# A long-convolution kernel: spectrum rows with real and imaginary part side by side, one transfer per chunk's multiplier, and taps stored in partition order

## The chip, the cores and the metric

The kernel runs on one core of a Trainium2 chip. The metric is device time in microseconds (us) of one execution; lower is better. A core has five engines that run side by side, each with its own instruction queue that is worked through in order: TensorE (PE, matrix products; PEld is its weight load), VectorE (DVE), ScalarE (ACT), GpSimd (POOL) and SyncE (SP). SP computes nothing here: it issues almost every transfer between the chip's DRAM and the on-chip memory, which has 128 partitions. The transfers themselves are carried out by 16 DMA engines; the profile's "DMA share" is the mean busy share of these 16.

## The reference

`x` has 2048 positions and 512 channels. Four layers are applied in turn, A, B, A, B, with the same weights for both A layers and both B layers, each added to `x`.

```python
def _A_ref(q, k, v, shift_k, ssm_k, ssm_D):      # q = layernorm(x)
    kv = shift_conv(k, shift_k) * v              # 4 taps per channel
    y = irfft(rfft(kv, 4096) * rfft(ssm_k, 4096))[:2048]
    return q * (y + kv * ssm_D)

def _B_ref(u, ...):                              # u = layernorm(x)
    K = 2 * real(sum_n C[d, n] * exp(A[d, n] * dt[d] * l))   # 512 channels x 2048 taps
    y = irfft(rfft(u, 4096) * rfft(K, 4096))[:2048]
    return y + u * D_skip

x = x + _A_ref(layernorm(x), ...); x = x + _B_ref(layernorm(x), ...)
x = x + _A_ref(layernorm(x), ...); x = x + _B_ref(layernorm(x), ...)
```

So there are long convolutions with two sets of filters, done as a product of spectra. The convolution in A does not depend on `x` (only its gate does), so it is computed once and used in both A layers. The convolution in B runs twice.

## The kernel before

**Tiling.** The 512 channels are handled in 4 quarters `q` of 128, each quarter in 4 groups `g` of 32. A 4096-point transform is done as two steps of small matrix products on TensorE. Step one (`pf`, line 177) is followed by a 32x32 block transpose on DVE; step two (`pu`, line 206, in `f2_pair`) gives the spectrum in 8 chunks `c` per quarter. A chunk is a block of 128 partitions by 4 residues by 128 channels. Of the 128 partitions one half belongs to a residue of one kind and the other half to the other kind; within a half, 32 rows hold real parts and the next 32 rows hold imaginary parts. The table `w2` sets this order. The way back is `i1_pair` (`pi`, line 221, with the table `mm`), a copy on ACT (line 341), a transpose on DVE (`w`, line 355) and a last product (`po`, line 361).

**The filters' spectra.** `spectrum_quarter` transforms the filter taps in the same way and stores the result chunk by chunk in DRAM (`spec`, line 290). For A (`which == 0`) the taps are an input. For B (`which == 1`) `taps()` computes them, group by group, with ACT, DVE, POOL and PE; `contract` scales them into a tile `ks` (lines 578 and 579), stores them to `kdram` (line 581), and `spectrum_quarter` loads them back into the tile `kk` (line 265). This last load goes through `by_half` (line 227): the positions in DRAM are in the order (a, b, n) and the tile wants (b, a, n), so it is done as two transfers of 64 partitions, and the DRAM side of each is a pattern of 2 blocks by 32 rows. `by_half` also loads the other inputs (`kk` for A, `kvt`, `xt`, `xr`) and stores the result (`out`, line 921).

**The convolution.** `convolution` runs through 32 chunks (4 quarters by 8). For each chunk, `load` (line 299) brings the filter's spectrum into a tile `kab` with two halves: `kab[:, 0]` are the rows as stored, `kab[:, 1]` the same rows with real and imaginary parts exchanged. The first takes one transfer of 256 KB (line 305), the second four of 64 KB (line 309). Then DVE forms `vv = pu * kab[:, 0]` (line 329), ACT copies `pu` (line 327) and POOL multiplies the copy by `kab[:, 1]` (line 328, `sw`). The matrix `mm` puts the four products of real and imaginary parts together with the right signs while it does the first inverse step. The inverse of a chunk pair runs `lag` chunks later, and the last inverse step another 8 chunks later; at its end `finish_b` (line 908) adds the result to `x` and, in the last layer, stores it.

**What sets the order.** The tile framework lets a program write tiles; it places the waits and, by its own simulation of the engines, orders the instructions of each queue. A tile name has a fixed number of buffers, and a new tile waits until the oldest is free: `kab` has 4 buffers in B (`NKB`) and is loaded 3 chunks ahead (`AHB`), 3 buffers and 2 chunks ahead in A; `yo`, the output tile in the last layer, has 3. Completion of a transfer issued on SP is counted on one of 8 counters in turn, and a transfer that gets a counter waits on SP until the one that had it before is done.

**Stages.** Up to about 466 us: inputs for A are loaded, A's filters are transformed, `kv` is formed, and the taps of B begin. From about 530 to 860 us: A's convolution, with B's taps running beside it; the taps end at about 917 us. From 942 us: B for the first time ("the first B round"). From about 1050 us: the second A layer, which is only its gate. From 1098 us: B for the second time ("the second B round").

## Time and profile before

| | |
|---|---|
| median of 3 runs | 1252.41 us (1247.11 to 1254.38) |
| the profiled execution, its own time | 1260.55 us |
| its span in the trace | 1258.7 us |
| busy: PE, PEld, DVE, ACT, POOL | 693.5, 453.6, 582.5, 412.8, 389.0 us |
| mean granted TensorE clock | 0.718 |
| moved by DMA | 147.49 MB in 93626 packets |
| issues of `kab <- spec` on SP | 94 of 256 KB and 376 of 64 KB |
| issues of `kk <- kdram` on SP | 32 of 128 KB |

No engine is busy for more than 55% of the span, so the time is not read from these shares but stage by stage. The views used below: "windows" give the busy time of each engine in a stretch, with instruction counts, the granted clock, the DMA share and the bytes moved; "timeline" lists the instructions of one engine in order (start, duration, what; in brackets the idle time before and what ended it); "waits" sum the idle time of an engine by what it waited for; "the chain of waits" follows the work that ended last back from its end. An issue on SP is shown as SPq with the time that the issuing took. The profiled execution lasted 8.1 us longer than the median.

### The profile page before, as it was taken

The numbers are of one execution on the slowest core, as the hardware profiler recorded it, in microseconds if no ns is written. First come the engines' busy times: TensorE is split into PE (matmuls) and PEld (weight loads), VectorE is DVE, ScalarE is ACT, GpSimd is POOL, SyncE is SP. The second block draws the span as 40 slices with busy tenths as digits, with TensorE's granted clock in tenths as the row PEclk, the third lists the DMA queues.
The fourth block names the chain that finished last, engine by engine and source line by source line (L and its number), as shares of the span: only waits on it lengthen the run. The fifth ranks groups of instructions, "written<-read, shape, count | busy, mean of one in ns | idle before, by whom it ended". The sixth has DMA issues, their size and how long they took to land. (4 is left out here: it accounts for less than half of the span.)

```text
span 1258.7 us, 21783 instructions
## 1 busy us (share of the span) xinstructions
PE 693.5 (55%) x8648; PEld 453.6 (36%) x8648; DVE 582.5 (46%) x995; ACT 412.8 (33%) x755; POOL 389.0 (31%) x371
## 2 busy tenths in 40 slices
PE   1220334143445455882455989987648884786651
PEld 0120213022323233551232757654435552354430
DVE  3320132445534323551215648786615668964330
ACT  2100131031213121571234454657325334752210
POOL 2331233443323211451113335432324341242220
PEclk9555566556656556796676979896768897897885
DMA  4112331222222233362335556446236763063431
GB/s 131 73 65 99 125 119 59 90 69 78 88 95 74 71 111 113 107 179 72 98 106 167 180 162 197 123 154 178 68 124 185 212 201 106 14 203 116 133 93 48
DMA packets 93626, 147.49 MB, mean 117 GB/s; under 512 B 12492, under 2 KB 41684, under 8 KB 90964
## 3 DMA queue, kind: packets, MB, share of 16 engines
q1 hardware_dynamic: 92532, 143.68, 35.7%
q0 software_dynamic: 992, 2.43, 0.6%
q8 instruction: 68, 1.11, 0.4%
q14 instruction: 34, 0.28, 0.1%
HBM read 102.01 MB, written 44.04 MB: 116 GB/s over the span
## 5 line engine op out<-in xcount | busy, mean ns | idle before, releaser
L328 POOL TENSOR_TENSOR sw<-sw,kab 128x512 f32<-128x512 f32 x96 | 121.9, 1276 | 293.9 <-DMA kab<-spec 155.4
L177 PE MATMUL pf<-kk,wz 128*128 128x256 f32 x256 | 106.2, 568 | 185.4 <-DMA kk<-ssmk_in 60.8
L206 PE MATMUL pu<-zk,w 64*64 64x128 f32 x1024 | 74.3, 349 | 137.6 <-ACT pc L289 95.2
L177 PEld LDWEIGHTS pf<-kk,wz 128*128 128x128 f32 x256 | 66.6, 281 | 213.7 <-issue 106.2
L329 DVE TENSOR_TENSOR vv<-pu,kab 128x512 f32<-128x512 f32 x96 | 64.1, 683 | 143.8 <-ACT sw L327 89.3
L289 ACT COPY pc<-pu 128x512 f32<-128x512 f32 x64 | 36.5, 587 | 284.1 <-DMA spec<-pc 174.2
L221 PE MATMUL pi<-vv,mm 64*64 64x128 f32 x1536 | 113.5, 289 | 6.7 <-DVE vv L329 4.2
L554 POOL TENSOR_TENSOR xy<-tt,m 128x512 f32<-128x512 f32 x64 | 86.8, 1356 | 91.7 <-issue 53.2
L206 PEld LDWEIGHTS pu<-zk,w 64*64 64x64 f32 x1024 | 58.0, 174 | 156.8 <-ACT pc L289 99.3
L221 PE MATMUL pi<-sw,mm 64*64 64x128 f32 x1536 | 109.7, 283 | 1.8 <-issue 1.6
L206 PE MATMUL pu<-zu,w 64*64 64x128 f32 x1536 | 90.0, 313 | 32.3 <-DVE yo L919 15.1
L206 PEld LDWEIGHTS pu<-zu,w 64*64 64x64 f32 x1536 | 72.0, 155 | 62.1 <-DVE vv L329 17.9
L660 DVE TENSOR_TENSOR u<-kvt 128x512 f32<-128x512 f32 x15 | 10.4, 693 | 175.7 <-DMA kvt<-kv_in 147.7
L221 PEld LDWEIGHTS pi<-vv,mm 64*64 64x64 f32 x1536 | 77.0, 141 | 36.9 <-issue 12.0
L327 ACT COPY sw<-pu 128x512 f32<-128x512 f32 x96 | 53.6, 590 | 97.9 <-PE pu L206 97.6
L541 ACT ACTIVATE tt<-pa 128x512 f32<-128x512 f32 x64 | 38.3, 601 | 139.6 <-PE pa L533 130.4
L661 POOL TENSOR_TENSOR tb<-kvt 128x512 f32<-128x512 f32 x16 | 27.6, 1728 | 177.3 <-DMA kvt<-kv_in 177.3
L221 PEld LDWEIGHTS pi<-sw,mm 64*64 64x64 f32 x1536 | 79.7, 141 | 4.3 <-issue 3.7
L197 DVE STREAM_TRANSPOSE zk<-pf 128x512 f32<-128x512 f32 x64 | 44.3, 703 | 67.3 <-PE pf L177 67.3
L361 PE MATMUL po<-w,w 128*64 128x512 f32 x192 | 59.0, 705 | 25.9 <-DVE vv L329 19.1
L569 PE MATMUL pk<-xy,tt 128*32 128x64 f32 x2048 | 58.5, 258 | 24.3 <-POOL tb L661 13.2
L518 ACT ACTIVATE m<-pm 128x512 f32<-128x512 f32 x96 | 54.2, 598 | 51.5 <-PE pm L516 50.2
(144 smaller groups left out, 1289.8 us busy)
## 6 DMA issues: line engine op xcount, KB each, us to landing
kab<-spec SPq DMA_DIRECT2D x94, 256.0 KB
kab<-spec SPq DMA_DIRECT2D x376, 64.0 KB
spec<-pc SPq DMA_DIRECT2D x64, 256.0 KB
kvt<-kv_in SPq DMA_DIRECT2D x32, 312.0 KB
kk<-ssmk_in SPq DMA_DIRECT2D x32, 128.0 KB
xr<-x_in SPq DMA_DIRECT2D x8, 512.0 KB
kv_d<-u SPq DMA_DIRECT2D x16, 256.0 KB
kdram<-ks SPq DMA_DIRECT2D x64, 64.0 KB
```

Source lines behind the costliest of these rows:

```text
L177: yield T.matmul(o, w, rhs, start=True, stop=True)
L197: V.transpose(zr, both)
L206: ins = T.matmul(pus[odd][64 * o:64 * o + 64, i, :], w2[64 * h:64 * h + 64, k, :], z[64 * h:64 * h + 64, :, k, :], start=True, stop=True, ...
L221: ins = T.matmul(pis[odd][64 * o:64 * o + 64, i, :], mm[64 * h:64 * h + 64, k + i, 64 * part:64 * part + 64], w[part][64 * h:64 * h + 64, ...
L327: swapped[0] = S.copy(wb, pu)
L328: G.tensor_mul(wb, wb, kabs[s][:, 1])
L329: V.tensor_mul(wa, pu, kabs[s][:, 0])
L361: ins = T.matmul(po[64 * a:64 * a + 64], w4, ws[g][:, :, 16 * a:16 * a + 16, :].rearrange("p x t r -> p t x r"), start=True, stop=True, ti ...
L518: i = S.activation(m, pm, AF.Exp)
L541: S.activation(co, rv, AF.Abs)
L554: G.tensor_mul(xy[:, :, :, 32:64], tt[:, :, :, 1:33], m1[:, :, 32:64][:, None].to_broadcast([128, 2, 8, 32]))
L569: T.matmul(pk[32 * i4:32 * i4 + 32, 2 * k + i, :], e2[:, r, 4 * i + i4, :], xy[:, r, 4 * i + i4, :], start=r == 0, stop=r == 1, tile_posit ...
```

## The change

Three things are changed together.

1. **Order of rows in the spectra.** In `w2` (and in `mm`, which takes the products apart again) the index of real or imaginary part is now innermost: rows 2f and 2f+1 are the real and the imaginary part of one frequency f. This order holds for the signal's spectrum (`pu`) and for the filter's (`spec`).
2. **One transfer per chunk's multiplier.** `kab[:, 0]` is now the filter's real part in both rows of a frequency, `kab[:, 1]` its imaginary part in both rows. So `vv = pu * Kre` and `sw = pu * Kim`, and `mm` has other signs and positions. In DRAM the two rows of a frequency lie one behind the other, 4096 bytes in all, and both rows of the tile get these same 4096 bytes. One transfer does it, with a source pattern of 64 by 2 (step 0) by 1024 elements; it moves 512 KB, as the five did.
3. **Taps in partition order.** `contract` writes `ks` so that the taps arrive in `kdram` in the order (b, a, n) of the partitions. The two multiplications keep their 256 elements per partition, with one more dimension in the pattern. `kk` is then loaded for B by one transfer of 128 partitions.

```diff
--- before.py
+++ after.py
@@ -35,8 +35,8 @@
     pos = (2 * n1[None, :] + a[:, None]).reshape(64)
     w1 = np.zeros((64, 2, 2, 32))
     w4 = np.zeros((2, 2, 32, 64))
-    w2 = np.zeros((2, 2, 32, 32, 2, 32))
-    mm = np.zeros((2, 2, 32, 32, 2, 2, 32))
+    w2 = np.zeros((2, 2, 32, 32, 32, 2))
+    mm = np.zeros((2, 32, 2, 32, 2, 2, 32))
     for k in range(32):
         for s in range(2):
             if k == 0 and s == 0:
@@ -46,13 +46,13 @@
                 for i in range(32):
                     r = i // 16
                     th = 2 * np.pi * ((128 * i if r == 0 else 64 + 128 * (i - 16)) * j % NFFT) / NFFT
-                    w2[0, r, :, 0, 0, i] = np.cos(th)
-                    w2[0, r, :, 0, 1, i] = -np.sin(th) if i else (-1.0) ** j
+                    w2[0, r, :, 0, i, 0] = np.cos(th)
+                    w2[0, r, :, 0, i, 1] = -np.sin(th) if i else (-1.0) ** j
                     if i == 0:
-                        mm[0, 0, 0, 0, 0, 0], mm[0, 1, 0, 0, 0, 0] = 1, (-1.0) ** j
+                        mm[0, 0, 0, 0, 0, 0], mm[0, 0, 1, 0, 1, 0] = 1, (-1.0) ** j
                     else:
-                        mm[0, 0, i, 0, 0, r], mm[0, 1, i, 0, 0, r] = 2 * np.cos(th), -2 * np.cos(th)
-                        mm[0, :, i, 0, 1, r] = -2 * np.sin(th)
+                        mm[0, i, 0, 0, 0, r], mm[0, i, 1, 0, 0, r] = 2 * np.cos(th), -2 * np.sin(th)
+                        mm[0, i, 0, 0, 1, r], mm[0, i, 1, 0, 1, r] = -2 * np.sin(th), -2 * np.cos(th)
                 continue
             f = k + 64 * s if k else 32
             ang = 2 * np.pi * (f * pos % 128) / 128
@@ -60,11 +60,13 @@
             w4[s, 0, k], w4[s, 1, k] = 2 * np.cos(ang) / NFFT, -2 * np.sin(ang) / NFFT
             th = 2 * np.pi * ((f + 128 * q)[None, :] * j[:, None] % NFFT) / NFFT
             co, si = np.cos(th), np.sin(th)
-            w2[s, 0, :, k, 0], w2[s, 0, :, k, 1] = co, -si
-            w2[s, 1, :, k, 0], w2[s, 1, :, k, 1] = si, co
-            mm[s, 0, :, k, 0, 0], mm[s, 0, :, k, 0, 1] = co.T, si.T
-            mm[s, 1, :, k, 0, 0], mm[s, 1, :, k, 0, 1] = -co.T, -si.T
-            mm[s, :, :, k, 1, 0], mm[s, :, :, k, 1, 1] = -si.T, co.T
+            w2[s, 0, :, k, :, 0], w2[s, 0, :, k, :, 1] = co, -si
+            w2[s, 1, :, k, :, 0], w2[s, 1, :, k, :, 1] = si, co
+            co, si = co.T, si.T
+            mm[s, :, 0, k, 0, 0], mm[s, :, 0, k, 0, 1] = co, si
+            mm[s, :, 1, k, 0, 0], mm[s, :, 1, k, 0, 1] = -si, co
+            mm[s, :, 0, k, 1, 0], mm[s, :, 0, k, 1, 1] = -si, co
+            mm[s, :, 1, k, 1, 0], mm[s, :, 1, k, 1, 1] = -co, -si
     for c in range(1, NCH, 2):
         odd = slice(CK * c, CK * c + CK)
         mm[:, :, :, odd] = mm[::-1, :, :, odd].copy()
@@ -262,7 +264,10 @@
         nc.sync.dma_start(dr, (ssmd_in, dsk_in)[which][:, 128 * q:128 * q + 128])
         for g in range(4):
             kk = pool.tile([128, 512], F32, name="kk", tag="kk", bufs=(NKK, 2)[which])
-            by_half(kk, src[4 * q + g])
+            if which == 0:
+                by_half(kk, src[4 * q + g])
+            else:
+                nc.sync.dma_start(kk, src[4 * q + g])
             d = dr[:, 32 * g:32 * g + 32]
             if which == 0:
                 kv = kk.rearrange("p (t c) -> p t c", c=32)
@@ -301,12 +306,8 @@
             pool = pools["conv"]
             kab = pool.tile([128, 2, CK, 128], F32, name="kab", tag="kab", bufs=nk)
             eng = G if first_b and s < GL else nc.sync
-            rows = spec[which][q][c]
-            eng.dma_start(kab[:, 0].rearrange("p k c -> p (k c)"), rows)
-            for r in range(2):
-                for h in range(2):
-                    o = 64 * h + 32 * r
-                    eng.dma_start(kab[o:o + 32, 1].rearrange("p k c -> p (k c)"), rows[64 * h + 32 - 32 * r:64 * h + 64 - 32 * r])
+            rows = spec[which][q][c].rearrange("(f v) x -> f (v x)", v=2)
+            eng.dma_start(kab.rearrange("p v k c -> p (v k c)"), rows[:, None, :].to_broadcast([64, 2, 2 * CK * 128]))
             kabs[s] = kab
 
         for s in range(-2 * NCH, NS + lag + NCH + 1):
@@ -573,10 +574,11 @@
             return
         q, g = divmod(gi, 4)
         ks = wk.tile([128, 64, 8], F32, name="ks", tag="ks", bufs=2)
-        d2 = dt2[:, q, 8 * g:8 * g + 8][:, :, None].to_broadcast([128, 8, 32])
-        kv_ = ks.rearrange("p n c -> p c n")
-        V.tensor_mul(kv_[:, :, 32:64], pk[:, :, 0:32], d2)
-        V.tensor_mul(kv_[:, :, 31::-1], pk[:, :, 32:64], d2)
+        d2 = dt2[:, q, 8 * g:8 * g + 8][:, :, None, None].to_broadcast([128, 8, 2, 16])
+        kv_ = ks.rearrange("p (b a t) c -> p a c b t", b=2, a=2)
+        halves = lambda m0: pk[:, :, m0:m0 + 32].rearrange("p c (b t) -> p c b t", b=2)
+        V.tensor_mul(kv_[:, 1], halves(0), d2)
+        V.tensor_mul(kv_[:, 0, :, ::-1, ::-1], halves(32), d2)
         for i4 in range(4):
             nc.sync.dma_start(
                 kdram[gi].rearrange("(s n) (i x) -> i n s x", n=32, i=4)[i4],
```

What is issued on the queues changes with it. The number of transfers of `kab <- spec` falls from 480 (470 on SP, 10 on POOL) to 96 (94 and 2), that of `kk <- kdram` from 32 to 16. Line numbers move by one to five. The order on SP at three places follows; a row is a line of the program, the operation, the tiles (left the destination) and the shape of the destination, and x2 stands for two in a row.

**SP, before the last loads of `xt`.** `xt` are the rows of `x` from which the first layernorm's sums are taken, and the stage up to 466 us ends with them. Before:

```order
L231 DMA xt<-x_in 64x1x512 x2
L290 DMA spec_3_60<-pc 128x512
L231 DMA xt<-x_in 64x1x512
L670 DMA kv_d_97<-u 128x512
L290 DMA spec_3_60<-pc 128x512
L231 DMA xt<-x_in 64x1x512 x5
L309 DMA kab<-spec_0_57 32x512
L305 DMA kab<-spec_0_57 128x512
```
Now:

```order
L233 DMA xt<-x_in 64x1x512 x2
L672 DMA kv_d_97<-u 128x512
L233 DMA xt<-x_in 64x1x512 x2
L295 DMA spec_3_60<-pc 128x512
L270 DMA kk<-kdram_67 128x512
L295 DMA spec_3_60<-pc 128x512
L233 DMA xt<-x_in 64x1x512 x2
L295 DMA spec_3_60<-pc 128x512
L233 DMA xt<-x_in 64x1x512 x2
L270 DMA kk<-kdram_68 128x512
L295 DMA spec_3_60<-pc 128x512
L233 DMA xt<-x_in 64x1x512
```
Two loads of `kk` from `kdram` (the groups 67 and 68) that came after the last `xt` now stand among the last ones; each is one row of 128 partitions.

**SP, end of the taps.** `kdram_80` is the last group of taps; its spectrum (`spec_3`) is stored, and then the first B round's loads begin. Before:

```order
L581 DMA kdram_79<-ks 32x4x128 x4
L231 DMA kk<-kdram_79 64x1x512 x2
L581 DMA kdram_80<-ks 32x4x128 x4
L231 DMA kk<-kdram_80 64x1x512 x2
L290 DMA spec_3_64<-pc 128x512 x8
L305 DMA kab<-spec_0_61 128x512
L309 DMA kab<-spec_0_61 32x512 x4
```
Now:

```order
L583 DMA kdram_79<-ks 32x4x128 x4
L270 DMA kk<-kdram_79 128x512
L583 DMA kdram_80<-ks 32x4x128 x4
L270 DMA kk<-kdram_80 128x512
L295 DMA spec_3_64<-pc 128x512 x8
L310 DMA kab<-spec_0_61 128x1x1024 x6
```
The order of the steps is the same; each load of `kk` is one issue, and the loads of `kab` that follow are one issue each.

**SP, the second B round, around the first stores of the result.** Before:

```order
L305 DMA kab<-spec_2_63 128x512
L309 DMA kab<-spec_2_63 32x512 x4
L305 DMA kab<-spec_2_63 128x512
L309 DMA kab<-spec_2_63 32x512 x4
L231 DMA out_dram<-yo 2x32x512 x2
L305 DMA kab<-spec_2_63 128x512
L309 DMA kab<-spec_2_63 32x512 x4
L305 DMA kab<-spec_2_63 128x512
L309 DMA kab<-spec_2_63 32x512
L231 DMA out_dram<-yo 2x32x512 x2
L309 DMA kab<-spec_2_63 32x512 x3
L231 DMA out_dram<-yo 2x32x512 x2
```
Now:

```order
L310 DMA kab<-spec_0_61 128x1x1024 x4
L310 DMA kab<-spec_1_62 128x1x1024 x8
L310 DMA kab<-spec_2_63 128x1x1024 x2
L233 DMA out_dram<-yo 2x32x512 x2
L310 DMA kab<-spec_2_63 128x1x1024 x2
L233 DMA out_dram<-yo 2x32x512 x4
L310 DMA kab<-spec_2_63 128x1x1024 x2
L233 DMA out_dram<-yo 2x32x512 x2
```
The stores keep their two issues per group (by halves). Ahead of the first store stood ten issues for two chunks, now two.

## The prediction

> **What bounds the kernel now.** I read the windows by stage first: time, the five engines' busy time, granted clock, DMA share, GB/s.
>
> ```profile
> 0.00:466.00 466.00, 159.48 (x1237) 101.48 (x1238) 165.40 (x216) 84.64 (x142) 148.46 (x143) 0.59 0.25 90
> ...
> 680.00:860.00 180.00, 158.81 (x2149) 106.44 (x2149) 132.24 (x247) 96.78 (x171) 72.16 (x69) 0.89 0.49 158
> 860.00:942.00 82.00, 49.99 (x563) 36.13 (x564) 35.09 (x65) 35.40 (x70) 23.59 (x29) 0.68 0.40 117
> 942.00:1036.00 94.00, 77.46 (x1390) 51.98 (x1388) 58.27 (x106) 41.58 (x87) 37.01 (x30) 0.89 0.66 202
> ...
> 1098.00:1259.00 161.00, 92.62 (x1580) 60.94 (x1578) 62.02 (x84) 40.70 (x80) 42.18 (x34) 0.80 0.39 119
> ```
>
> Only from 680 to 860 us is an engine near full: PE, 159 of 180 us. Up to 466 us no engine passes 36%. The two B rounds do nearly the same work (1390 and 1580 products), yet one takes 94 us for its chunks and the other 161 us to the end. So three stages wait for something that is no engine. What it is, narrow windows and issues show:
>
> ```profile
> 303.00:313.00 10.00, 10.00 (x83) 5.29 (x82) 5.56 (x9) 4.31 (x8) 2.35 (x2) 0.70 0.14 54
> 1242.00:1258.00 16.00, 0.00 (x0) 0.00 (x0) 0.69 (x1) 0.00 (x0) 0.00 (x0) 0.50 0.12 48
> 274.98 6.03 SPq L231 DMA_DIRECT2D kk<-kdram  x2
> 456.11 10.23 SPq L231 DMA_DIRECT2D xt<-x_in  x5
> kvt<-kv_in SPq DMA_DIRECT2D x32, 312.0 KB
> kk<-ssmk_in SPq DMA_DIRECT2D x32, 128.0 KB
> xt<-x_in SPq DMA_DIRECT2D x32, 128.0 KB
> ```
>
> Where transfers by halves (`by_half`) run alone, loads at 303 us or the last stores from 1242 us, the DMA share stays at 0.12 to 0.14: 0.125 is two engines of sixteen, and they move 48 to 54 GB/s. A pair of halves, 256 KB, thus holds two engines for 4.9 to 5.5 us. The three loads by halves before 466 us (32 x 312 KB and 64 x 128 KB, 18.6 MB) need 345 to 390 us at that rate, and an issue on SP takes microseconds there since SP waits for earlier transfers. **The early stage is bound by two DMA engines.** The first B round shows another picture in the chain of waits (start, duration, what):
>
> ```profile
> 963.85 0.36 SPq L305
> 964.25 0.43 SPq L309
> 964.72 0.42 SPq L309
> 965.18 0.42 SPq L309
> 965.65 0.42 SPq L309
> 966.18 0.36 SPq L305
> POOL sw L328 <- DMA kab<-spec: 58.2, 23, 15.9
> DVE vv L329 <- DMA kab<-spec: 18.3, 9, 5.2
> ```
>
> One chunk's five issues take 2.33 us (963.85 to 966.18), with stalls 94/32 = 2.94 us, and the chain runs through them issue after issue; POOL and DVE wait for `kab` (the last two rows, the waits from 930 to 1060 us: in total, times, longest). **The first B round is bound by SP's issuing.** The second round has both: the same issues, and the stores by halves among them.
>
> ```profile
> 1126.78 0.65 DVE L919 TENSOR_TENSOR yo<-x,po 128x512 f32<-128x512 f32 x1
> 1135.98 1.15 SPq L231 DMA_DIRECT2D out_dram<-yo  x2
> 1145.38 0.69 DVE L919 TENSOR_TENSOR yo<-x,po 128x512 f32<-128x512 f32 x1 [7.77 <-DMA out_dram<-yo]
> DVE yo L919 <- DMA out_dram<-yo: 33.6, 5, 8.2
> SPq L309 <- DMA out_dram<-yo: 12.8, 8, 3.8
> ```
>
> The first `yo` is done at 1127.4, but its store is issued at 1136.0, behind ten issues of `kab`; the fourth `yo` wants its buffer and DVE stands 7.8 us, with PE behind it. Loads wait for stores in turn, since there are 8 counters.
>
> **The change, part by part.** All sums are against the profiled execution (1260.55 us, of which 1258.7 us span); it lies 8.1 us above the median, and I carry the difference over to the median unchanged.
>
> *Products and rows.* `vv` and `sw` keep their shapes, `w2` and `mm` theirs: 0. The two scalings of the taps get a pattern with one more dimension:
>
> ```profile
> L578 DVE TENSOR_TENSOR ks<-pk,dt x16: 580/613/654, 268.7 to 916.8; 128x256 f32<-128x256 f32 x16
> L579 DVE TENSOR_TENSOR ks<-pk,dt x16: 623/640/681, 269.1 to 917.2; 128x256 f32<-128x256 f32 x16
> ```
>
> The second is already the odder pattern (it writes backwards) and costs 27 ns more. I take 0; if every one of the 32 grew by half its time it would be 10 us of DVE, of which only the last group's 0.6 us lies on the chain.
>
> *One load of `kk` for two halves (16 pairs).* The last groups stand on the chain, with nothing beside them:
>
> ```profile
> 899.58 7.00 DMA kk<-kdram
> 921.61 7.54 DMA kk<-kdram
> POOL kk L275 <- DMA kk<-kdram: 60.8, 12, 11.1
> PE pf L177 <- DMA kk<-kdram: 30.9, 6, 12.6
> 907.20 3.75 PE L177 MATMUL pf<-kk,wz 128*128 128x256 f32 x8 [5.09 <-DMA kk<-kdram]
> SPq L581 <- DVE ks L579: 46.5, 7, 17.7
> kab<-spec POOLq DMA_DIRECT2D x2, 256.0 KB, 3.2
> kab<-spec POOLq DMA_DIRECT2D x8, 64.0 KB, 2.6
> ```
>
> A 256 KB transfer over 128 partitions landed in 3.2 us when POOL issued it; SP's own have no landing time, so I take 3.2. That gives 3.8 + 4.3 = **8 us** at the end of the taps (bounds 4, if the load at 899 is covered by the taps' ACT work, and 9). Before 466 us two pairs go off the two engines: 2 x (4.9 - 0.6, the same bytes over sixteen) = 8.6; but SP also stands for the taps themselves (46.5 us at line 581), when the two engines can run dry, so **7 us** (0 to 9); the two loads that now stand ahead of the last `xt` cost 0.6 us each. Of the ten pairs between, PE waited 30.9 - 12.6 - 5.1 = 13 us; half of that goes: **6 us** (0 to 13). What is late next there is `xr` and PE itself, which stays full from 680 to 860 us.
>
> *One load of `kab` for five.* SP's 2.33 us per chunk become one issue. Nearest rows: 0.36 us for 128 rows, and 1.30 us for the only load with a repeated dimension, made among others at the start:
>
> ```profile
> L467 SPq DMA_DIRECT2D dt<-ldtb_in x1: 1302/1302/1302, 4.4 to 4.4; - x1
> ```
>
> I take 0.4, by the row of nearer shape; even 1.3 is under PE's share of a chunk. So SP leaves the chain of the first B round, and the next bound is PE, at full clock:
>
> ```profile
> 1116.93 0.88 PE pu L206 x32
> 1117.81 1.06 PE pf L177 x4
> 1118.87 1.92 PE pi L221 x64
> 1041.38 1.08 PE po L361 x4
> ```
>
> 16 pairs x 3.86 + 16 groups x 1.08 = 79 us against 94. The transfers need 32 x 512 KB / 202 GB/s = 83 us at today's share of 0.66, so some 55 us when full. PE will not run without gaps (the clock in this stage was 0.89): **10 us** (0 to 17, the latter PE's busy 77.5 of 94). POOL's eight issues less at 927 us lie beside the last taps' load: 0. `vv` now waits for 512 KB, no longer for the first 256; with loads 3 chunks (8 us) ahead this is covered, and without that cover it costs 0.8 us per chunk (2.6 and 3.2 us for 64 and 256 KB give 4.0 for 512).
>
> A rule speaks against this term. The Trainium skill, "DMA: Bandwidth & Descriptors", section "Issuing engines are not separate DMA queues", says that the time a sequencer needs to start a DMA is usually small beside the DMA itself. By it the SP terms of both B rounds would be nothing and the sum 21 instead of 44. Here the rows above have 2.33 us of issue beside 2.6 us of data per chunk (512 KB at 202 GB/s), so I go by the rows.
>
> *Second B round.* Stores remain by halves. The first `yo` comes at about 1125 (1126.8 less a stall of `vv`), is stored at once, and from there the two engines carry 16 x 5.5 = 88 us of stores and some 16 chunks x 32 KB at 24 GB/s each = 22 us of loads: 1125 + 110 + 2 = 1237 if they never idle. Before, 1136 + 88 + 14 x 1.37 = 1243 stands against 1258.7, 16 us of idling. I keep half of that idling: 1246, **13 us** (0 to 23). What is late next are the two engines.
>
> *A's convolution* (560 to 860 us): its loads of `kab` shrink too, but PE or `xr` is the bound there: 0 (-8 to 8, since the order on all queues shifts).
>
> Sum: 8 + 7 + 6 + 10 + 13 = 44 us: 1260.6 - 44 = 1216.6 profiled, and 1252.4 - 44 = **1208** for the median.
>
> **Rivals.**
>
> *Only the bare waits* (chance 0.20): the two engines set the early stage and the second B round whatever SP does, and gaps elsewhere close up. Left are 8 at the taps' end and 10 in the first round: 1234 us. For it: the stores keep their halves. Against it: the 8.6 us by which the first store came late.
>
> *All bounds met* (0.13): 9 + 9 + 13 + 17 + 23 + 5 (A) = 76, 1176 us. For it: PE's idle time behind SP is plain in both rounds. Against: it needs PE without gaps.
>
> *Both products wait for one landing* (0.06): place `vv` and `sw` in all 96 chunks, price 0.8 us each, 77 us; less the 44 it is +33, 1285 us. It decides from the point at which a load is issued less than 4 us before its chunk's `pu` is copied. For it: `vv` waits for `kab` today (9 times in the first round). Against: those waits come from SP's issuing.
>
> *The load does not spread* (0.03): like the halves, the new source has a dimension of 2, and if it ran on two engines a chunk would take 512 KB / 54 GB/s = 9.7 us instead of 2.9, some 650 us more over three rounds, 1900 us. Against: in the halves the 2 is outermost, here 64 is. The Trainium skill, the same page, section "Why a DMA increments its semaphore by 16 and not by 1", says that the number of engines is the largest up to 16 that divides the slowest dimension of both sides; by it the halves get 2 and this load 16. For the halves the trace agrees (0.12 to 0.14); for a load of this shape no run here shows it yet.
>
> **How the numbers follow.** The forecast has 0.58; its own range from the bounds is 1186 to 1228. 8 in 10 need the first rival and most of the second: 1176 to 1242. A measurement of this kernel tells about 0.5% (6 us) from no change. Faster: all of the forecast but 0.02, 0.17 of the first rival, the second: 0.86. Same: 0.05. Slower: the two last rivals: 0.09.
>
> **What would show it.** Right: issues of `kab` of about 0.4 us and gaps between them on SP from 942 us; POOL's and DVE's waits for `kab` in the first round (58 and 18 us) mostly gone, PE without idle time; `kk` landing in 3 to 4 us on the chain; the first store within 2 us of its `yo`; the window after the last `yo` still at 0.12. Wrong: SP still on the chain, a DMA share near 0.13 while `kab` loads run, or a first B round that is not shorter.

## The result, and the profile after

The changed kernel takes 1166.79 us (median of 4 runs, 1157.36 to 1169.77) against 1249.76 us (4 runs, 1245.26 to 1254.38) for the kernel before: a ratio of 0.932, 95% interval 0.926 to 0.939. The gain is 83 us; the forecast was 44 us, and 1166.79 lies below the range of 1176 to 1242. The profiled execution of the changed kernel took 1169.77 us, its span 1167.9; that is 90.8 us under the span before, and the stages below are cut out of these two spans.

A stage is marked by the start of an instruction that both timelines have: the statistics of the last `xt`, the first product of A's convolution on POOL (`sw`), the `ks` of the last taps but one, and `sw` of chunk 0, of chunk 31 and of the second round's chunk 0. The last column is the prediction's term; its 6 us "in between" were for all loads of `kk` from there to the taps' end, and for the second A layer it had no term.

| stretch | before | after | difference | forecast |
|---|---|---|---|---|
| start to the last `xt` | 479.1 | 470.1 | -9.0 | -7 |
| to A's first product | 49.2 | 26.2 | -23.0 | -6 (the loads "in between") |
| to the `ks` of the last taps but one | 365.8 | 366.6 | +0.8 | 0 |
| to the first round's first product | 54.2 | 40.9 | -13.3 | -8 |
| first B round, to its chunk 31 | 91.7 | 72.9 | -18.8 | -10 |
| second A layer | 57.1 | 58.3 | +1.2 | none |
| second B round, to the end | 161.7 | 133.0 | -28.7 | -13 |

No term of the sum has the wrong sign; three are about two to four times too small. The windows of the changed kernel at the B rounds (columns as before: PE, PEld, DVE, ACT, POOL, then clock, DMA share, GB/s):

```profile
904.00:977.00 73.00, 69.45 (x1380) 47.83 (x1382) 58.35 (x107) 36.39 (x73) 39.28 (x32) 0.95 0.70 247
...
1061.00:1152.00 91.00, 62.60 (x1072) 39.53 (x1070) 43.52 (x57) 24.45 (x46) 25.39 (x20) 0.86 0.37 132
1152.00:1168.00 16.00, 0.00 (x0) 0.00 (x0) 0.32 (x1) 0.00 (x0) 0.00 (x0) 0.50 0.11 45
```

and the same stretches of the kernel before:

```profile
948.00:1040.00 92.00, 77.48 (x1424) 53.36 (x1426) 59.64 (x108) 36.86 (x75) 39.57 (x32) 0.89 0.65 197
...
1127.00:1242.00 115.00, 67.95 (x1058) 43.98 (x1056) 42.58 (x55) 24.59 (x46) 26.74 (x21) 0.80 0.36 111
```

In the first B round PE is now busy for 69.5 of 73 us: PE bounds it in the main. In the second round PE is busy for only 62.6 of 91 us, and the last 16 us still run at a DMA share of 0.11: two engines of sixteen. The waits of the changed kernel from 903 to 977 us, and the line shares of its chain of waits from 904 to 977 us, say the same:

```profile
DVE vv L330 <- DMA kab<-spec: 4.1, 2, 2.1
...
POOL sw L329 <- DMA kab<-spec: 2.2, 2, 1.4
```

```profile
by line: PE pi L223 25.4%; PE pu L208 19.2%; PE po L362 14.1%; PE pf L179 10.2%; issue 8.1%; DMA kab<-spec 7.9%; ACT ie L342 4.4%; DVE vv L330 3.7%; DVE w L356 3.4%; POOL sw L329 1.8%; DVE zu L197 1.1%; ACT sw L328 0.8%; DVEq L330 0.1%; POO
```

POOL waited 58.2 us for `kab` in the row shown of before, now 2.2; no issue on SP is among the lines shown of the chain. One issue of the new load takes 0.54 us on SP when nothing holds it. From 904 to 977 us SP waits for products to free a buffer of `kab`, 40.0 us for `vv` and 12.0 us for `sw`; six loads then take 13.53 us:

```profile
497.57 0.54 SPq L310 DMA_DIRECT2D kab<-spec  x1
943.70 13.53 SPq L310 DMA_DIRECT2D kab<-spec  x6
```

### The profile page after: what moved, and what is told of

Read it like the earlier page. It is cut to its first block, busy times and chain, and to the rows that moved or that the text cites. A ratio compares the mean times of both kernels' runs of the same rounds, so it can differ in the third digit from the quotient of the medians.

```text
span 1167.9 us, 21248 instructions
## 1 busy us (share of the span) xinstructions
PE 669.5 (57%) x8648; PEld 441.8 (38%) x8648; DVE 582.7 (50%) x995; ACT 412.3 (35%) x755; POOL 388.7 (33%) x363
## 4 chain that ended last, share of the span: by engine, by line
DMA 39%; PE 22%; SPq 12%; DVE 10%; issue 7%; ACT 6%; POOL 3%; DVEq 0%; ACTq 0%; POOLq 0%
DMA kvt<-kv_in 9%; PE pi L223 7%; SPq L233 7%; DMA spec<-pc 5%; DMA xr<-x_in 5%; DMA xt<-x_in 5%; PE pf L179 5%; PE pu L208 4%; DMA kk<-ssmk_in 4%; DMA kab<-spec 3%; PE po L362 3%; DMA u<-kv_d 3%; DMA out_dram<-yo 2%; PE pk L570 1%; PE pm L517 1%
## 5 line engine op out<-in xcount | busy, mean ns | idle before, releaser
L179 PE MATMUL pf<-kk,wz 128*128 128x256 f32 x256 | 102.2, 550 | 125.4 <-DMA kk<-ssmk_in 56.3
L208 PE MATMUL pu<-zk,w 64*64 64x128 f32 x1024 | 72.2, 341 | 134.8 <-ACT pc L294 90.8
L223 PE MATMUL pi<-vv,mm 64*64 64x128 f32 x1536 | 116.0, 290 | 34.9 <-DVE vv L330 29.1
L208 PEld LDWEIGHTS pu<-zk,w 64*64 64x64 f32 x1024 | 55.5, 168 | 151.0 <-ACT pc L294 94.2
L208 PE MATMUL pu<-zu,w 64*64 64x128 f32 x1536 | 82.9, 292 | 7.8 <-DVE vv L330 4.7
L556 DVE TENSOR_TENSOR tt<-tt,m 128x512 f32<-128x512 f32 x64 | 66.8, 1045 | 30.6 <-ACT tt L544 30.0
L208 PEld LDWEIGHTS pu<-zu,w 64*64 64x64 f32 x1536 | 65.2, 142 | 36.6 <-DVE vv L330 14.7
L517 PE MATMUL pm<-tg,rw 64*128 64x512 f32 x96 | 48.1, 586 | 52.9 <-ACT m L519 52.9
L223 PEld LDWEIGHTS pi<-sw,mm 64*64 64x64 f32 x1536 | 77.5, 141 | 2.2 <-issue 2.2
L328 ACT COPY sw<-pu 128x512 f32<-128x512 f32 x96 | 53.4, 589 | 56.0 <-PE pu L208 55.3
L570 PE MATMUL pk<-xy,tt 128*32 128x64 f32 x2048 | 53.4, 250 | 28.8 <-POOL tb L663 18.9
```

What stands on the lines that cost most here:

```text
L179: yield T.matmul(o, w, rhs, start=True, stop=True)
L208: ins = T.matmul(pus[odd][64 * o:64 * o + 64, i, :], w2[64 * h:64 * h + 64, k, :], z[64 * h:64 * h + 64, :, k, :], start=True, stop=True, ...
L223: ins = T.matmul(pis[odd][64 * o:64 * o + 64, i, :], mm[64 * h:64 * h + 64, k + i, 64 * part:64 * part + 64], w[part][64 * h:64 * h + 64, ...
L328: swapped[0] = S.copy(wb, pu)
L517: mt = T.matmul(pm, rows[gi][hs, 1, :], rhs, start=True, stop=True)
L556: (G if (4 * gi + k) % E2P == E2P - 1 else V).tensor_mul(e2, e2, m2[:, None].to_broadcast([128, 2, 8, 32]))
```

## The experiments

All run times are medians, and ratios are to the kernel before. The stretches of the table above, in the profiled execution of each kernel:

| | last `xt` | A's first product | `ks`, last but one | first round | its chunk 31 | second A | end |
|---|---|---|---|---|---|---|---|
| before | 479.1 | 49.2 | 365.8 | 54.2 | 91.7 | 57.1 | 161.7 |
| taps alone | 472.3 | 26.8 | 356.0 | 46.0 | 86.9 | 56.5 | 160.8 |
| multipliers alone | 478.6 | 46.9 | 361.6 | 56.2 | 72.4 | 58.3 | 133.8 |
| after | 470.1 | 26.2 | 366.6 | 40.9 | 72.9 | 58.3 | 133.0 |
| five transfers | 470.9 | 27.1 | 341.7 | 42.2 | 106.5 | 55.1 | 170.2 |
| two transfers | 471.1 | 25.5 | 353.6 | 46.9 | 73.0 | 57.5 | 139.2 |
| `kk` forced ahead, halves | 495.3 | 30.9 | 365.0 | 48.2 | 88.4 | 56.7 | 161.9 |
| `kk` held behind, one load | 472.2 | 28.4 | 341.2 | 41.5 | 72.5 | 58.3 | 133.9 |
| `kk` in two loads, spread | 470.3 | 36.1 | 337.2 | 44.7 | 73.7 | 57.5 | 134.0 |
| result spread | 472.9 | 26.5 | 353.5 | 45.4 | 72.7 | 57.5 | 95.7 |
| all halves spread | 224.7 | 22.9 | 280.2 | 44.0 | 73.1 | 58.5 | 95.2 |
| before, all halves spread | 236.2 | 32.5 | 296.9 | 45.4 | 88.1 | 55.3 | 118.7 |

### Which part gives which stage: one part at a time

The kernel before with the third part of the change alone, and the changed kernel without it:

```diff
-            by_half(kk, src[4 * q + g])
+            if which == 0:
+                by_half(kk, src[4 * q + g])
+            else:
+                nc.sync.dma_start(kk, src[4 * q + g])
...
+        V.tensor_mul(kv_[:, 1], halves(0), d2)
+        V.tensor_mul(kv_[:, 0, :, ::-1, ::-1], halves(32), d2)
```

> The kernel before with the third part alone: taps in partition order, one load of kk; the multipliers still come by five transfers. Of the 91 us that the profiled execution lost, the early stage holds 9, the stretch from the last xt to A's convolution 23, the taps' end about 8, and the B rounds 47. Theory 1 (the 23 us belong to the loads of kk, which held the taps' chain there): 1250 - 9 - 23 - 8 = 1210 us, first POOL product of A's convolution near 497 us, both B rounds as before (92 us from sw 32 to sw 63). Theory 2 (the 23 us belong to the multipliers: their issues of five stand between the taps' loads and stores on SP): 1250 - 9 - 8 = 1233 us, and that first product near 519 us.

> The changed kernel without its third part: kk by halves, the old order of the taps, but one transfer per chunk's multiplier. Both theories: the B rounds gain what they gained, 18 + 29 = 47 us. Theory 1 (the 23 us between the last xt and A's convolution belong to kk): 1250 - 47 = 1203 us. Theory 2 (they belong to the multipliers): 1250 - 47 - 23 = 1180 us. If neither holds and the two parts only pay together, it comes out at or above 1203 and the run of the taps alone above 1225.

Taps alone: 1203.57 us (1198.56 to 1209.67), ratio 0.961 (0.956 to 0.966). Multipliers alone: 1207.88 us (1205.26 to 1213.24), ratio 0.965 (0.961 to 0.969). The 23 us between the last `xt` and A's first product belong to `kk` (-22.4 in the one kernel, -2.3 in the other), both B rounds in the main to the multipliers (-19.3 and -27.9; with the taps alone -4.8 and -0.9). Theory 1 holds, theory 2 falls. Apart, the parts win 49.5 + 45.2 = 95 us, together 83: the 12 us are lost mainly in A's stretch, the third column (-9.8 and -4.2 apart, +0.8 together); the last section shows what may move it.

### Is it the number of issues on SP

The changed kernel, its rows as they are, with a multiplier in five transfers, and in two:

```diff
-            rows = spec[which][q][c].rearrange("(f v) x -> f (v x)", v=2)
-            eng.dma_start(kab.rearrange("p v k c -> p (v k c)"), rows[:, None, :].to_broadcast([64, 2, 2 * CK * 128]))
+            rows = spec[which][q][c].rearrange("(f v) x -> f v x", v=2)
+            eng.dma_start(kab[:, 0].rearrange("p k c -> p (k c)"), rows[:, 0][:, None, :].to_broadcast([64, 2, CK * 128]))
+            for r in range(4):
+                eng.dma_start(kab[32 * r:32 * r + 32, 1].rearrange("p k c -> p (k c)"),
+                              rows[16 * r:16 * r + 16, 1][:, None, :].to_broadcast([16, 2, CK * 128]))
```

```diff
-            rows = spec[which][q][c].rearrange("(f v) x -> f (v x)", v=2)
-            eng.dma_start(kab.rearrange("p v k c -> p (v k c)"), rows[:, None, :].to_broadcast([64, 2, 2 * CK * 128]))
+            rows = spec[which][q][c].rearrange("(f v) x -> f v x", v=2)
+            for v in range(2):
+                eng.dma_start(kab[:, v].rearrange("p k c -> p (k c)"), rows[:, v][:, None, :].to_broadcast([64, 2, CK * 128]))
```

> The changed kernel with its new rows, but the multiplier of a chunk fetched by five transfers again (one of 128 rows, four of 32 partitions, rows of 2 KB). Theory (the number of issues on SP is what the B rounds gained by): the first round is back at 92 us for its chunks 32 to 63 (73 with one transfer) and the second loses about as much as it won, so 1167 + 18 + 29 = 1214 us or somewhat less. Rival (what paid is the larger packet, 4 KB in place of 2 KB, or the layout of the rows): packets are 2 KB here as in the next kernel, and both come out alike, above 1180 us. Rival (the gain is elsewhere): near 1167 us.

> The changed kernel with the multiplier of a chunk in two transfers, one per product row, 2 KB packets. Theory (issues count): two issues of 0.42 us are 0.9 us per chunk, under the 2.3 us in which PE goes through one, so 1167 to 1175 us. Rival (packet size): as with five transfers, above 1180 us. The first product no longer waits for the whole 512 KB, so a gain of up to some 5 us from the earlier half is possible too.

Five transfers: 1218.20 us (1215.50 to 1225.72), ratio 0.973 (0.969 to 0.978). Two: 1167.47 us (1161.74 to 1172.00), ratio 0.931 (0.926 to 0.936), the same as one. Both have 2 KB packets and the new rows, so neither the packet nor the layout is the cause: the number of issues is, as the theory says. Five are dearer here than before, 106.5 us for the first round against 91.7: an issue with a repeated source row takes 0.55 us and more; the timeline of SP in that round (start, duration, count) and POOL's wait from 882 to 988 us:

```profile
933.70 0.55 SPq L310 DMA_DIRECT2D kab<-spec  x1
934.29 2.50 SPq L312 DMA_DIRECT2D kab<-spec  x4
```

```profile
POOL sw L332 <- DMA kab<-spec: 47.9, 20, 5.4
```

With 3 us and more of issues per chunk SP is the bound again. Two issues of that price, 1.1 us, stay under the 2.3 us (73/32) that PE needs. This also answers the rival of one landing for both products: with two transfers the first product waits for 256 KB only, and the time is the same.

### What gives the 23 us: the engines, or the order on SP

In the kernel before the third and the fourth `kk` of the taps are issued behind the last `xt`, in the changed kernel ahead of it. POOL's first touch of these two tiles (it adds D to one row as soon as they are loaded), before:

```profile
485.89 0.24 POOL L275 TENSOR_TENSOR kk<-kk,dr 1x32 f32<-1x32 f32 x1 [5.33 <-DMA kk<-kdram]
496.55 0.24 POOL L275 TENSOR_TENSOR kk<-kk,dr 1x32 f32<-1x32 f32 x1 [8.63 <-PE pf L177]
```

and after:

```profile
452.85 0.24 POOL L280 TENSOR_TENSOR kk<-kk,dr 1x32 f32<-1x32 f32 x1 [10.96 <-DMA kk<-kdram]
465.82 0.24 POOL L280 TENSOR_TENSOR kk<-kk,dr 1x32 f32<-1x32 f32 x1 [12.73 <-DMA kk<-kdram]
```

Three kernels take this apart. In the first, the kernel before has its last `xt` ordered behind the halves of the fourth `kk` (`kks` holds the last issue of each `kk` of the taps):

```diff
-            by_half(xt, x_in[:, t, :])
+            ins = by_half(xt, x_in[:, t, :])
+            if t == 15:
+                after(ins, kks[3])
```

In the second, the changed kernel has the third and fourth `kk` ordered behind the last `xt`:

```diff
-            by_half(xt, x_in[:, t, :])
+            ins = by_half(xt, x_in[:, t, :])
+            if t == 15:
+                after(kks[2], ins)
+                after(kks[3], ins)
```

In the third, the changed kernel loads each `kk` of the taps by two transfers of 64 partitions in partition order:

```diff
-                nc.sync.dma_start(kk, src[4 * q + g])
+                for b in range(2):
+                    nc.sync.dma_start(kk[64 * b:64 * b + 64], src[4 * q + g][64 * b:64 * b + 64])
```

> The kernel before, but its last xt load is ordered on SP behind the fourth kk load of the taps (in the changed kernel the third and the fourth kk stand ahead of the last xt; before, both stand behind it). Theory O (the 23 us between the last xt and A's convolution come from this order: before, the kk loads stand on SP among waiting issues): 1253 - 23 + 5, some 1235 us, with the first POOL product of A's convolution near 510 us instead of 528. Theory L (they come from the load itself, which ran as halves on two of 16 DMA engines): no gain, 1253 us or a few more.

> The changed kernel, but its third and fourth kk load are ordered on SP behind the last xt load, as they stood before the change. Theory O (the order gave the 23 us): 1167 + 23 = 1190 us, first product of A's convolution near 519 us. Theory L (the load over 16 engines gave them): 1167 us, first product near 497 us, and the two kk land in 3 to 5 us instead of 10 to 12.5.

> The changed kernel with each kk load of the taps in two transfers of 64 partitions, both in partition order. This has the two issues of the kernel before, and its order on SP (the third and fourth kk behind the last xt), but the source has 64 rows as its slowest dimension, not 2. Theory L (engines): 1167 to 1175 us. Theory O (order): 1190 us. Rival (what paid at the taps' end was one issue for two): the load on the chain after the last taps stays above 6 us and the time is 8 us above 1167 or more.

Order alone: 1247.27 us (1241.67 to 1254.12), ratio 0.994 (0.990 to 0.998). Held behind: 1152.67 us (1148.86 to 1156.64), 0.918 (0.913 to 0.924). Two loads, spread: 1156.96 us (1153.01 to 1160.62), 0.922 (0.916 to 0.928). In the first kernel the halves put ahead push the last `xt` from 479 to 495 us and win only 2 us at A's first product: without the spread that order is worth next to nothing. In the second the loads behind the last `xt` lose little (28.4 us from there to A's first product, against 26.2), though from issue to POOL's touch they still took 11 to 12 us, not 3 to 5. But this is not their place before. There, as in the third kernel, they stood behind three loads of `u` (the rows that A's convolution transforms) as well, and the third of these waits for the last `xt`, whose buffer it takes: in all five kernels of the table below it is issued 0.7 us after the last `xt` is touched. The order on SP in the second and then in the third kernel:

```profile
460.52 3.37 SPq L273 DMA_DIRECT2D kk<-kdram  x2
463.98 0.56 SPq L698 DMA_DIRECT2D u<-kv_d  x1
```

```profile
465.42 5.96 SPq L693 DMA_DIRECT2D u<-kv_d  x2
471.43 1.14 SPq L271 DMA_DIRECT2D kk<-kdram  x2
```

So the clean comparison for the engines is the third kernel with that of the multipliers alone, where `kk` stands at the same place in two issues but comes by halves: 36.1 us from the last `xt` to A's first product against 46.9, 10.8 of the 23. Another 9.9 (36.1 to 26.2) come with the place on SP or with one issue for two, which were not tried apart, and 2.3 with the multipliers (49.2 to 46.9). Theory O falls as a cause by itself, but theory L gives about half, not the whole.

PE runs the last transforms of the fourth `kk` (`pf`, from 499.1 us before, 473.5 after) just ahead of those of the second `u` (503.7 and 476.5), so A's first product comes behind two things: the last `xt`, which lets the third `u` be loaded, and the fourth `kk`. The start of A's convolution moves with the later of the two (times of the first touch by DVE and POOL):

| | last `xt` | fourth `kk` | A's first product | after the later of the two |
|---|---|---|---|---|
| before | 479.1 | 496.6 | 528.3 | 31.7 |
| halves, ahead | 495.3 | 490.2 | 526.1 | 30.8 |
| two loads, spread | 470.3 | 478.4 | 506.5 | 28.1 |
| one load, behind | 472.2 | 474.0 | 500.7 | 26.7 |
| after | 470.1 | 465.8 | 496.3 | 26.2 |

The last column varies by 5.5 us, that of the fourth `kk` by 31. The fourth `kk` came 17.5 us after the last `xt` before; held behind, it comes 1.7 us after, in the changed kernel 4.3 us ahead. These 17.5 us and the 5.5 of the last column are the 23. With the multipliers alone, where `kk` still comes by halves, the two are 14.0 us apart (478.6 and 492.6) and A's first product follows 32.9 us after the later one, as before.

### The two engines that are left

The changed kernel with the result stored by four transfers of 32 partitions per tile, and then with every transfer by halves (`kvt`, `kk` of A, `xt`, `xr`, the result) done so:

```diff
         for b in range(2):
-            ends = tile_[64 * b:64 * b + 64], src[b]
-            nc.sync.dma_start(*(ends[::-1] if store else ends))
+            for a in range(2):
+                o = 64 * b + 32 * a
+                ends = tile_[o:o + 32], src[b][a]
+                nc.sync.dma_start(*(ends[::-1] if store else ends))
```

> The changed kernel, but each of the 16 result tiles is stored by four transfers of 32 partitions in place of two halves of 64. Theory (the stores by halves hold two DMA engines of sixteen, and these bound the second B round from the first store on): the 16 us from the last yo to the end shrink to 3 or 4, and DVE's waits for a free yo go, so 1167 - 12 - 5 to 15 = 1140 to 1150 us. Rival (only the end shrinks, since PE or SP bounds the round before it): 1155 us. Rival (the four transfers run on the same engines, or SP's two more issues per tile cost what is won): 1167 us or more.

> The changed kernel with every remaining transfer by halves (the inputs kvt, kk of A, xt, xr and the result) as four transfers of 32 partitions. Theory (two DMA engines of sixteen bound the early stage, and the four xr loads that the chain shows with 28 us each): no engine is busy for more than 165 of the first 466 us, so the stage can shrink until SP's issues, the taps or an engine with its dependences bind it; at 100 to 200 us less there, 4 x 20 less for xr and 15 to 25 less in the second B round the time would be some 870 to 1050 us. Rival (the early stage waits for something else, such as the taps' chain through ACT and DVE): 1167 - 80 - 20, 1065 us or more. Rival (transfers of 32 partitions don't spread either): 1167 us.

Result alone: 1126.38 us (1124.37 to 1128.29), ratio 0.899 (0.892 to 0.905), below the 1140 to 1150 that were expected. All: **805.92 us** (800.34 to 807.59), ratio 0.643 (0.638 to 0.649), below the range that was expected. The windows of these two, first the one with the result alone:

```profile
1056.00:1117.00 61.00, 55.89 (x1066) 36.34 (x1062) 41.87 (x56) 24.20 (x46) 25.32 (x20) 1.00 0.64 195
1117.00:1124.00 7.00, 0.00 (x0) 0.00 (x0) 0.69 (x1) 0.00 (x0) 0.00 (x0) 0.75 0.46 111
```

```profile
0.00:224.00 224.00, 150.02 (x1397) 97.80 (x1397) 191.11 (x239) 91.12 (x156) 161.57 (x150) 0.74 0.68 196
```

From the first `yo` to the last, 61 us in place of 91, the clock at 1.00 in place of 0.86 and PE busy for 56 us of it: with sixteen engines the second round is PE's too. The stage to the last `xt` shrinks from 470 to 225 us, and DVE, 35% busy in the kernel before, is now busy for 85% of it. The four loads of `xr` take up to 28 us each in the chain of the changed kernel (the row below); from the first to the last normalization of `xr` 50.7 us pass with all halves spread, 115.9 in the changed kernel.

```profile
532.33 27.85 DMA xr<-x_in
```

The same edit to the kernel before tells what the change is worth when the two engines bind no more:

> The kernel before with every transfer by halves (kk of A and B, kvt, xt, xr, the result) as four transfers of 32 partitions. Beside the changed kernel with the same edit (806 us) it tells what the change is worth where the two DMA engines are no bound. Theory: the multipliers' issues still bind the B rounds, +18 in the first; in the second the gain over five issues is 17 to 20 as well, since PE binds it then; kk in four is spread, so nothing there: 806 + 38 = 844 us. Rival (SP, with five issues per chunk and four per input tile, becomes the bound of the early stages too): 870 us or more. Rival (no difference left): 806 us.

872.06 us (865.75 to 874.99), ratio 0.694 (0.689 to 0.698), 66 us over 805.92. The theory's 844 us is missed, the rival comes nearest. Of the 74.6 us between the two spans, 15.0 and 23.5 lie in the B rounds and 39.3 ahead of the first, where the rival puts five issues a chunk and four a tile on SP; the second A layer gives 3.2 back. That SP's issues make the 39.3 is not shown: 16.7 of them lie in A's stretch, which moves with the order of the queues too.

Last, the inputs and the result are laid out in DRAM in the order (b, a, n), so that each pair of halves becomes one transfer; the second of these kernels also has the multiplier in two transfers, by the edit shown above.

```diff
-        src = rows.rearrange("(a b n) y -> b a n y", a=2, b=2)
-        for b in range(2):
-            ends = tile_[64 * b:64 * b + 64], src[b]
-            nc.sync.dma_start(*(ends[::-1] if store else ends))
+        nc.sync.dma_start(*((rows, tile_) if store else (tile_, rows)))
...
-    return np.asarray(a).reshape(32, 2, 2, 16, -1).transpose(1, 2, 0, 3, 4).reshape(128, 16, -1)
+    return np.asarray(a).reshape(32, 2, 2, 16, -1).transpose(2, 1, 0, 3, 4).reshape(128, 16, -1)
```

> The changed kernel, with the inputs kvt, kk of A, xt and xr and the result laid out in DRAM in the partition order (b, a, n), so that each transfer by halves becomes a single one of 128 partitions. Theory (what paid with four transfers of 32 partitions, 806 us, was the number of DMA engines; SP's issues are no bound any more, since the chain there is PE 17%, DVE 10%, SPq 1%): within some 20 us of 806. Rival (four issues per tile cost something in the first 224 us): 780 us or less. Rival (large single transfers are worse than four small ones): 830 us or more.

> As the last one, with the multiplier of a chunk in two transfers, one per product row. With the halves gone, the chain in the first B round runs for 16% through the landing of a multiplier of 512 KB. Theory (the landing of the whole 512 KB holds up the first product): some 5 to 10 us less than the last one. Rival (loads 3 chunks ahead cover it): the same within 5 us.

The first took 806.32 and 809.99 us in two runs (span of the latter 808.2, against 798.6 with four transfers) and 822.17 and 823.08 us in two others, so no ratio is given. The second took 813.31 us (811.91 to 814.00), ratio 0.648 (0.646 to 0.649). The theory holds that the number of engines is what pays, by one transfer or by four; the multiplier in two transfers gains nothing, so its landing is covered. The lowest median is that of the kernel with four transfers, 805.92 us.

## Why the prediction was wrong, point by point

**What bounds the kernel** was read rightly in all three stages: SP in the first B round (five against two transfers), two engines in the early stage and at the end (225 us in place of 470, 7 in place of 16).

**Products and rows, 0:** right. The two scalings of `ks` in the changed kernel (shortest, median, longest in ns):

```profile
L580 DVE TENSOR_TENSOR ks<-pk,dt x16: 578/618/659, 266.8 to 877.9; 128x256 f32<-128x256 f32 x16
L581 DVE TENSOR_TENSOR ks<-pk,dt x16: 624/643/686, 267.3 to 878.3; 128x256 f32<-128x256 f32 x16
```

**`kk` to the last `xt`, 7:** 9.0 measured, 6.8 in the kernel with the taps alone. Right.

**`kk` in between, 6:** 23. **This is the step that failed most.** It took the wait from PE's row (30.9 us over all), although the row beside it gave POOL 60.8 us for the same loads, and POOL's touch stands ahead of PE's product. And it knew that two loads now stand ahead of the last `xt`, but priced them only as a delay of 0.6 us each; the place, or the single issue, is worth 9.9 us. The question it did not ask: which of two inputs comes last in front of A's convolution? Before it was the fourth `kk`, by 17.5 us.

**`kk` at the taps' end, 8 (4 to 9):** 13.3 here; 7.3 to 12.7 in the six other kernels of the table with the single or spread load and the inputs by halves (8.2 with the taps alone). The term is of the right size, its upper bound was too low. Of the 13.3, 7.9 us are won ahead of the last `ks`, 2.8 between it and POOL's touch of the last `kk`, where the prediction had 4.3, and 2.7 behind that. The last `kk` is touched 2.8 us after its issue, against 5.6 before (921.06 and 926.63). The timeline of the changed kernel:

```profile
882.17 0.34 SPq L270 DMA_DIRECT2D kk<-kdram  x1
884.93 0.24 POOL L280 TENSOR_TENSOR kk<-kk,dr 1x32 f32<-1x32 f32 x1 [8.28 <-DMA kk<-kdram]
```

**`kab`, first B round, 10 (0 to 17):** 18.8. The direction and SP's part were right, the next bound was mis-sized. **PE's floor of 79 us is the step that failed here.** It counted the products of a whole round, 16 pairs and 16 groups, against a stretch of 94 us that holds fewer. PE's lines in that stretch, from 942 to 1036 us before:

```profile
L206 PE MATMUL pu<-zu,w 64*64 64x128 f32 x474 | 26.6, 306 | 11.1 <-DVE vv L329 8.0 <-DVE zu L195 3.1
L221 PE MATMUL pi<-vv,mm 64*64 64x128 f32 x416 | 25.5, 292 | 0.1
L221 PE MATMUL pi<-sw,mm 64*64 64x128 f32 x416 | 24.9, 285 | 1.6 <-issue 1.6
L177 PE MATMUL pf<-u,w 64*128 64x512 f32 x48 | 17.3, 740 | 0.8 <-DVE zu L195 0.8
L361 PE MATMUL po<-w,w 128*64 128x512 f32 x36 | 10.0, 631 | 3.0 <-DVE vv L329 3.0
```

That is `pu` for 14.8 pairs (474/32), `pi` for 13 (832/64), 12 `pf` (48/4) and 9 `po` (36/4); at the prediction's own durations some 60 us. A floor of 79 also lay above PE's busy time in the stretch, 77.5 us, so it could not be one. Nor was the busy time, from which the upper bound of 17 came: in the changed kernel 69.5 us of 73 are left, at a granted clock of 0.95 in place of 0.89 and with a mean of 281 ns for a product of `pu` in place of 306, for nearly as many products (1380 and 1390). With two transfers it was 67.3 us at 0.98.

**`kab`, second B round, 13 (0 to 23):** 28.7. The bound was right to 4 us: from the first `yo` to the end 106.4 us are measured, 110 were worked out for two engines that never idle. The step that failed in this term is "I keep half of that idling". All of it went, and 3 us were won ahead of the first `yo`; its store follows at once:

```profile
1061.51 0.64 DVE L921 TENSOR_TENSOR yo<-x,po 128x512 f32<-128x512 f32 x1
1062.17 1.22 SPq L233 DMA_DIRECT2D out_dram<-yo  x2
```

**A's convolution, 0 (-8 to 8):** +0.8 here, but only by luck of the order, see below.

**The range.** The bounds of the five terms add up to 4 and 71 us, with A's 8 to either side of that. The narrower 1186 to 1228 us is not derived in the text, and the result lies below the 1176 at which all upper bounds were met: four upper bounds were too low, 9 and 13 us for `kk` and 17 and 23 for the B rounds.

**The rivals.** "Only the bare waits" fell with the B rounds. "All bounds met" (76 us, 1176) came nearest; it was given 0.13 for want of PE without gaps. "Both products wait for one landing" fell with the run of two transfers. "The load does not spread" fell with the share of 0.70 and the 247 GB/s of the first round; 512 KB issued by POOL landed in 4.1 us, where 4.0 were estimated:

```profile
kab<-spec POOLq DMA_DIRECT2D x2, 512.0 KB, 4.1
```

The stores by halves stay at a share of 0.11 in the last window, about the same bytes in patterns of 32 rows reach 0.46. The Trainium skill, "DMA: Bandwidth & Descriptors", section "Why a DMA increments its semaphore by 16 and not by 1", gives as the number of engines the largest up to 16 that divides the slowest dimension of both sides. The runs agree: 0.11 for a dimension of 2, more than 2/16 for 32 (0.46) and for the new load's 64 (0.70).

**The rule against it.** The Trainium skill, "DMA: Bandwidth & Descriptors", section "Issuing engines are not separate DMA queues", has the time to start a DMA usually small beside the transfer. With two issues per chunk the starts cost nothing that shows here (1167.47 us, as with one). With five of 0.55 us and more they do (1218.20 us).

## What to carry to other kernels

When a wait is taken away, list every input of the place where it ended, with the time each is there: what is won is about the distance to the next one (17.5 of the 23 us here), and it is not read from one engine's wait row when another engine stands in front. For a floor of an engine count the instructions that the stretch really holds; it is at most the engine's busy time there, and can come out lower still, as here, where PE's clock was higher afterwards (0.89 and 0.95). If a window shows a DMA share of 2/16 while work waits, look first at the shape of those transfers: here that was worth 361 us, four times this change.

## What had not been expected of the hardware

**A's convolution moves by 25 us with the order on ACT.** The stretch from A's first product to the `ks` of the last taps but one took 366.6 us in the changed kernel and 341.2 with two loads moved by a few places, though all its instructions are the same. ACT works in order, and the normalization of `xr` holds it while a load by halves comes in. In the changed kernel no copy for `sw` stands between the third and the fourth of these; POOL's product behind them starts at 638.11 us after 64.57 us without work:

```profile
597.03 2.93 ACT L713 ACTIVATE xr<-xr,nb,rs 128x512 f32<-128x512 f32 x4 [23.95 <-DMA kab<-spec]
...
634.15 2.92 ACT L713 ACTIVATE xr<-xr,nb,rs 128x512 f32<-128x512 f32 x4 [30.79 <-DMA u<-kv_d]
...
637.46 0.57 ACT L328 COPY sw<-pu 128x512 f32<-128x512 f32 x1
```

With the loads held behind, four copies stand there:

```profile
595.32 2.93 ACT L719 ACTIVATE xr<-xr,nb,rs 128x512 f32<-128x512 f32 x4 [20.57 <-DMA xr<-x_in]
...
599.58 1.06 ACT L331 COPY sw<-pu 128x512 f32<-128x512 f32 x2
...
607.96 1.07 ACT L331 COPY sw<-pu 128x512 f32<-128x512 f32 x2
631.78 2.92 ACT L719 ACTIVATE xr<-xr,nb,rs 128x512 f32<-128x512 f32 x4 [22.75 <-issue]
```

The twelfth chunk after the first has its product 177.7 us after A's first one in the changed kernel and 145.4 us with the loads held behind, so the whole difference arises here. This is read from two traces; no run moved these copies alone. So a change that touches the queues at all can win or lose 25 us and more in this stage (337 to 367 us over the kernels here with `xr` by halves), and a range of -8 to 8 for it was too narrow.

**An issue with a repeated source row costs more on SP:** 0.54 to 0.55 us against 0.36 us for the plain 128 rows of the kernel before.

**Single transfers are not better than four per tile.** From the start to A's first product the kernel with the new layout took 255.5 us, with four transfers of 32 partitions 247.5 (224.7 + 22.9), for the same bytes and a fourth of the issues. Whether the transfers or the order make the 8 us was not tried.
